# Loads of k, q and v of a pack-attention and soft-MoE kernel, issued as one transfer or as two

## The chip, the core and the metric

The kernel runs on one core of one Trainium2 chip. The metric is device time of one execution in microseconds (us). The kernel before takes 209.94 us (median of 3 runs, 209.9 to 210.69).

## What is computed

For each of 8 batches and 8 heads, with 576 rows of 64 numbers, 32 packing queries first attend to all keys and values, and then every row attends to the 32 packed results. The output, 4608 rows of 512 numbers, goes through a soft mixture of experts with 32 slots (8 experts of 4 slots).

```python
def sm_attn(qq, kk, vv):
    s = scale * np.matmul(qq, kk.transpose(0, 1, 3, 2))
    a = softmax(s)
    return np.matmul(a, vv)
p_packed = sm_attn(p, k, v)
x = sm_attn(q, p_packed, p_packed)          # then heads side by side: 4608 x 512
logits = x @ phi
slot_input = softmax(logits, axis=0).T @ x   # 32 slots
slot_out[e] = relu(slot_input[e] @ w1[e]) @ w2[e]
out = softmax(logits, axis=1) @ slot_out
```

All of it is in 32-bit floats.

## The kernel before

The attention is done in eight steps i, each for two batches (b2 = 0, 1) and four heads. A step needs six loads, two each of k, q and v, one for each b2. `rows9` (line 187) gives the source of such a load: head 4g + 2m + x, row 9r + t lies on partition 64x + r, at column 576m + 64t + d. So two heads (x) lie on the 128 partitions, two more (m) side by side in the columns, and each partition receives two runs of 576 numbers (2304 bytes), 294,912 bytes apart in memory. A load is 576 KB.

All loads stand in one list, `loads`, in the order p0; k, q, v of step 0; p1, p2, p3; k of step 1; four small pieces of phi; q and v of step 1; then k, q, v of steps 2 to 7; then the expert weights w1 and w2 (mostly 1024 KB each). `pump` (line 147) walks through this list as far as room allows and issues the transfers, all from SyncE (SP), whose queue is served in order. Most loads go into `ring`, a tile of 30,720 columns that is handed out from left to right and round again; a region is handed out again when its last reader has been recorded (`release`). `load` (line 136) issues one transfer for each load, at line 142; the pieces of phi are issued at line 151.

The order of all other work is written out by hand in `ORDER`, a list of tokens that name a function, a step and a part; each engine takes its instructions in that order. The tokens of this study: `kt` (line 395, VectorE) transposes a quarter of k of a step, and reads both halves m of the columns; `s1` (411) makes the first scores, and `mx1` (424) their maximum; `qp` (557) transposes q, in groups of columns 0 to 511, 512 to 639 and 640 to 1151; `ap` (444) transposes the first weights; `m` (466) multiplies by v, and reads both halves; `s2` (583), `mx2` (604) and `sb` (614) make the second scores, their maxima, and the difference; `p` (360) transposes the packing queries; `mp` (530) multiplies the packed results by phi; `w` (836) are products of ones that are not used, put into the order where TensorE would be idle. Steps overlap: `kt` of a step stands in the order among the second half of the step before.

Of the kernel before, what the change touches and what calls it, by code (L numbers as in the profile page):

```python
# [71 lines left out]
def pack_attention_soft_moe(  # L72
# [11 lines left out]
    nc = tc.nc  # L84

    B, H, S, D = q.shape
# [6 lines left out]
    T = S // R  # L93
# [42 lines left out]
    def load(dst, src):  # L136
        shape = src.shape[1:]
        if len(shape) == 2:
            dst = dst.rearrange("p (a b) -> p a b", a=shape[0])
        elif len(shape) == 3:  # L140
            dst = dst.rearrange("p (a b c) -> p a b c", a=shape[0], b=shape[1])
        nc.sync.dma_start(out=dst, in_=src)
# [4 lines left out]
    def pump():  # L147
        while state["next"] < len(loads):
            key, width, src = loads[state["next"]]
            if key == "phi":  # L150
                nc.sync.dma_start(out=width, in_=src)
                state["next"] += 1
                continue
            if key in spots:
                if spots[key] not in ready:
                    return
                dst = ready[spots[key]]
                where[key] = (dst, width)
                load(dst[:, 0:width], src)
                state["next"] += 1  # L160
                continue
            if "at" not in state:
                state["at"] = region(key, width)
            _, off, _ = state["at"]
            if not free(off, width):
                return
            regions.append(state.pop("at"))
            where[key] = (off, width)
            load(ring[:, off : off + width], src)
            state["next"] += 1  # L170
# [67 lines left out]
    for x in PLACE:  # L238
        key, width, src = extra.pop() if x == "x" else chunks.pop(0)
# [851 lines left out]
    for dd in range(ND):  # L1091
# [8 lines left out]
        for t in range(T):  # L1100
            n4, a = divmod(dd * T + t, 4)
# [57 lines left out]
```

## Time and profile before

| What | Before |
|---|---|
| Median of 3 runs | 209.94 us |
| The profiled execution | 211.11 us |
| its span (first to last instruction) | 209.0 us |
| TensorE busy (matmul) | 173.9 us, 83% of the span |
| VectorE, ScalarE, GpSimd busy | 125.4, 85.7, 39.1 us |
| Read from and written to memory | 62.46 MB, 9.44 MB |
| Share of the 16 DMA engines' time that the loads and stores took | 89.3% |

The profiled execution took 2.1 us more than its span, and 1.2 us more than the median. PE is TensorE's matmuls and PEld its weight loads; DVE is VectorE, ACT ScalarE, POOL GpSimd, SP SyncE. A releaser behind "<-" is what ended an idle time; "issue" is idle time in which the engine waited for nothing that the profile shows.

### The profile page before, as it was taken

The numbers are of one execution on the slowest core, as the hardware profiler recorded it, in microseconds if no ns is written. First come the engines' busy times: TensorE is split into PE (matmuls) and PEld (weight loads), VectorE is DVE, ScalarE is ACT, GpSimd is POOL, SyncE is SP. The second block draws the span as 40 slices with busy tenths as digits, with TensorE's granted clock in tenths as the row PEclk, the third lists the DMA queues.
The fourth block names the chain that finished last, engine by engine and source line by source line (L and its number), as shares of the span: only waits on it lengthen the run. The fifth ranks groups of instructions, "written<-read, shape, count | busy, mean of one in ns | idle before, by whom it ended". The sixth has DMA issues, their size and how long they took to land.

```text
span 209.0 us, 6539 instructions
## 1 busy us (share of the span) xinstructions
PE 173.9 (83%) x2827; PEld 110.1 (53%) x2827; DVE 125.4 (60%) x260; ACT 85.7 (41%) x205; POOL 39.1 (19%) x65
## 2 busy tenths in 40 slices
PE   7949779697898999999999998989989899796000
PEld 3625575593875858687858774543323323464000
DVE  1757488775749898977557799657742201387000
ACT  3063363394475847257377735031201000288000
POOL 7200006306442073002727001003000000000000
PEclk9999999999999999999999999999999999999555
DMA  6998999999999999955979999958999990069997
GB/s 210 386 383 283 395 393 391 389 389 389 389 390 391 388 396 405 408 205 182 346 292 389 408 407 420 420 219 278 427 425 422 419 384 14 3 265 411 410 417 302
DMA packets 23196, 72.31 MB, mean 346 GB/s; under 512 B 2176, under 2 KB 2944, under 8 KB 21248
## 3 DMA queue, kind: packets, MB, share of 16 engines
q1 hardware_dynamic: 23168, 71.90, 89.3%
q8 instruction: 22, 0.36, 0.7%
q14 instruction: 6, 0.05, 0.1%
HBM read 62.46 MB, written 9.44 MB: 344 GB/s over the span
## 4 chain that ended last, share of the span: by engine, by line
PE 60%; DVE 18%; ACT 8%; issue 7%; ACTq 0%; DVEq 0%
PE ps L583 9%; PE ps L466 7%; PE ps L836 7%; PE ps L1005 6%; PE ps L557 5%; PE ps L411 5%; PE ps L675 4%; PE ps L444 3%; ACT ring L345 3%; ACT work L345 2%; DVE mx L604 2%; PE ps L951 2%; DVE work L349 2%; PE ps L699 2%; DVE a L666 1%
## 5 line engine op out<-in xcount | busy, mean ns | idle before, releaser
L345 ACT COPY work<-ps 128x512 f32<-128x512 f32 (+3 forms) x64 | 28.9, 489 | 27.0 <-PE ps L557 12.8
L395 DVE STREAM_TRANSPOSE work<-ring 128x576 f32<-128x576 f32 x32 | 22.9, 752 | 2.8 <-DMA ring<-in_k_dram 2.6
L557 PE MATMUL ps<-ident,ring 128*128 128x128 f32 x144 | 20.8, 278 | 2.1 <-issue 1.9
L583 PE MATMUL ps<-work 128*64 128x64 f32 x576 | 20.1, 224 | 2.8 <-issue 2.4
L466 PE MATMUL ps<-ring,work 64*64 64x128 f32 x576 | 19.3, 274 | 2.2 <-ACT work L345 1.4
L583 PEld LDWEIGHTS ps<-work 128*64 128x64 f32 x576 | 18.4, 138 | 5.1 <-issue 3.9
L836 PE MATMUL ps<-ones 128*128 128x512 f32 (+3 forms) x40 | 19.2, 583 | 1.0 <-DVE ones L115 1.0
L466 PEld LDWEIGHTS ps<-ring,work 64*64 64x64 f32 x576 | 15.9, 133 | 5.2 <-ACT work L345 2.1
L557 PEld LDWEIGHTS ps<-ident,ring 128*128 128x128 f32 x144 | 15.9, 141 | 4.4 <-issue 3.1
L651 POOL TENSOR_TENSOR zt<-work 128x576 f32<-128x576 f32 x4 | 5.7, 1430 | 55.5 <-ACT work L643 55.5
L349 DVE COPY work<-ps 128x128 f32<-128x128 f32 (+3 forms) x28 | 13.0, 470 | 5.1 <-PE ps L557 1.9
L604 DVE TENSOR_REDUCE mx<-ps 128x36 f32<-128x1152 f32 x8 | 10.8, 1353 | 6.4 <-PE ps L583 6.2
L411 PE MATMUL ps<-work 32*32 32x288 f32 x512 | 13.4, 413 | 1.1 <-issue 0.9
L345 ACT COPY a2Tb<-ps 128x384 f32<-128x384 f32 x21 | 9.7, 481 | 10.8 <-PE ps L675 10.8
L427 ACT ACTIVATE work<-ps,nm 128x576 f32<-128x576 f32 x16 | 11.8, 741 | 4.5 <-DVE nm L424 4.5
L424 DVE TENSOR_REDUCE nm<-ps 128x2 f32<-128x1152 f32 x8 | 10.8, 1349 | 3.7 <-PE ps L411 3.7
L951 PE MATMUL ps<-ring,a2Tb 128*32 128x512 f32 x96 | 12.4, 594 | 0.4 <-DVE a2Tb L1017 0.4
L836 PEld LDWEIGHTS ps<-ones 128*128 128x128 f32 x40 | 7.2, 212 | 10.4 <-issue 9.2
L444 PE MATMUL ps<-ident,work 128*128 128x128 f32 x72 | 11.1, 277 | 1.5 <-ACT work L427 1.5
L1005 PE MATMUL ps<-ring,hT 128*32 128x512 f32 x88 | 11.4, 597 | 0.0
L345 ACT COPY ring<-ps 128x512 f32<-128x512 f32 (+1 forms) x21 | 10.4, 621 | 1.1 <-PE ps L1119 0.6
L654 POOL TENSOR_TENSOR zt<-zt 128x288 f32<-128x288 f32 (+2 forms) x18 | 10.5, 584 | 1.4
(138 smaller groups left out, 251.4 us busy)
## 6 DMA issues: line engine op xcount, KB each, us to landing
ring<-in_moe_w_dram SPq DMA_DIRECT2D x24, 1024.0 KB, 10.9
ring<-in_k_dram SPq DMA_DIRECT2D x16, 576.0 KB, 11.9
ring<-in_q_dram SPq DMA_DIRECT2D x16, 576.0 KB, 11.9
ring<-in_v_dram SPq DMA_DIRECT2D x16, 576.0 KB, 12.0
out_dram<-ring SPq DMA_DIRECT2D x10, 768.0 KB, 8.3
work<-in_moe_w_dram SPq DMA_DIRECT2D x6, 1024.0 KB, 11.2
a<-in_moe_w_dram SPq DMA_DIRECT2D x1, 1024.0 KB, 4.8
ring<-in_moe_w_dram SPq DMA_DIRECT2D x2, 512.0 KB, 18.0
```

The lines of the kernel that those rows point to most:

```text
L345: nc.scalar.copy(dst, src)
L349: nc.vector.tensor_copy(dst, src)
L395: nc.vector.transpose(kT[:, b2, :, c].rearrange("p m (t r) -> p m t r", t=T), view(f"k{i}.{b2}").rearrange("p (m t c d) -> p m t c d", m=2 ...
L411: nc.tensor.matmul(ps[32 * y : 32 * y + 32, banks["s1", i] + z, 0 : 32 * T], pT[rs, dd, b2, g, c, m], kT[rs, b2, m, c], start=(c == 0), st ...
L444: nc.tensor.transpose(ps[:, bank, o : o + P], a1[:, t].rearrange("p x r -> p (x r)"), ident)
L466: nc.tensor.matmul(ps[64 * b2 : 64 * b2 + 64, b + x, 0:P].rearrange("p (m d) -> p m d", m=2), a1T[rs, t, b2], view(f"v{i}.{b2}").rearrange ...
L557: nc.tensor.transpose(ps[:, bank, o : o + P], view(f"q{i}.{b2}")[:, P * n : P * n + P], ident)
L583: nc.tensor.matmul(psf[64 * b2 : 64 * b2 + 64, o + 64 * n : o + 64 * n + 64].rearrange("p (a s) -> p a s", a=2), qT[:, b2, n, 64 * x : 64 ...
L604: nc.vector.tensor_reduce(mxs[i % 2][:, a0:a1].rearrange("p a t -> p (a t)"), s2v(i, j).rearrange("p a t s -> p (a t) s"), axis=AX.X, op=A ...
L836: nc.tensor.matmul(ps[:, bank, 0 : P * n].rearrange("p (n c) -> p n c", n=n), ones, ones.unsqueeze(1).broadcast_to([P, n, P]), start=True, ...
L951: nc.tensor.matmul(ps[32 * a : 32 * a + 32, b + nh, :], xzf[:, (4 * e + a) * NSLOT : (4 * e + a + 1) * NSLOT], wv[:, j, nh * 512 : (nh + 1 ...
L1005: nc.tensor.matmul(ps[32 * a : 32 * a + 32, SO, :], hTf[:, (NJ * e + j) * NSLOT : (NJ * e + j + 1) * NSLOT], w2v(e, j), start=(e == 0 and ...
```

## The change

In `load`, a source of two rows of 576 numbers for each partition, which only the 48 loads of k, q and v have, is issued as two transfers, one for each m: 128 runs of 2304 bytes each, 288 KB, one behind the other in SP's queue. What is loaded, where it lies and the order of the list stay.

```diff
         if len(shape) == 2:
             dst = dst.rearrange("p (a b) -> p a b", a=shape[0])
+            if shape[0] == 2 and shape[1] == T * D:
+                for a in range(2):
+                    nc.sync.dma_start(out=dst[:, a], in_=src[:, a])
+                return
         elif len(shape) == 3:
             dst = dst.rearrange("p (a b c) -> p a b c", a=shape[0], b=shape[1])
         nc.sync.dma_start(out=dst, in_=src)
```

## Rows read from the trace of the kernel before

**Rows 1.** The page, parts 1 and 2: engines, and data moved in 40 slices.
```profile
PE 173.9 (83%) x2827; PEld 110.1 (53%) x2827; DVE 125.4 (60%) x260; ACT 85.7 (41%) x205; POOL 39.1 (19%) x65
...
GB/s 210 386 383 283 395 393 391 389 389 389 389 390 391 388 396 405 408 205 182 346 292 389 408 407 420 420 219 278 427 425 422 419 384 14 3 265 411 410 417 302
```

**Rows 2.** The chain that ended last, part of 18 to 56 us: start, us, what.
```profile
25.10 1.42 issue
...
29.53 1.32 DVE work L614
...
39.20 1.87 issue
...
47.59 0.90 issue
...
54.29 0.67 issue
```

**Rows 3.** Busy time and instructions (x) by stretch: us, PE, PEld, DVE, ACT, POOL.
```profile
41.00:48.48 7.48, 6.53 (x127) 5.61 (x127) 4.48 (x10) 5.59 (x12) 1.46 (x2) 1.00 1.05 387
48.48:54.95 6.47, 5.29 (x128) 3.73 (x128) 4.46 (x7) 2.78 (x8) 2.23 (x5) 1.00 1.05 390
```

**Rows 4.** The page, part 3: queue q8, its packets and MB.
```profile
q8 instruction: 22, 0.36, 0.7%
```

**Rows 5.** Packets by queue in the windows 48.49:52.30, 52.30:53.54, 91.0:94.24 and 94.24:95.6 us.
```profile
q1 hardware_dynamic: 682, 1.48, 104.8%
q14 instruction: 1, 0.01, 0.5%
...
q8 instruction: 1, 0.02, 6.2%
...
q1 hardware_dynamic: 80, 0.28, 22.5%
...
q8 instruction: 1, 0.02, 5.8%
```

**Rows 6.** PEld in order of time, near 93 us.
```profile
93.12 0.31 PEld L583 LDWEIGHTS ps<-work 128*64 128x64 f32 x6 [0.22 <-issue]
```

**Rows 7.** SP in order of time: start, us from first issue to end of the last.
```profile
0.73 0.38 SPq L142 DMA_DIRECT2D ring<-in_p_dram  x1
1.17 0.93 SPq L142 DMA_DIRECT2D ring<-in_k_dram  x2
...
14.26 1.25 SPq L151 DMA_DIRECT2D phi_sb<-in_moe_phi_dram  x2
15.55 1.11 SPq L142 DMA_DIRECT2D ring<-in_q_dram  x2
...
33.41 2.85 SPq L142 DMA_DIRECT2D ring<-in_k_dram  x2
```

**Rows 8.** Transfers issued at 0.73, 3.87, 18.82, 33.41, 154.27, 156.75 us: issue to landing.
```profile
DMA to landing us min/median/max: 2.1/2.1/2.1
...
DMA to landing us min/median/max: 10.4/10.4/10.4
...
DMA to landing us min/median/max: 8.6/8.6/8.6
...
DMA to landing us min/median/max: 12.0/12.0/12.0
...
DMA to landing us min/median/max: 18.6/18.6/18.6
...
DMA to landing us min/median/max: 17.4/17.4/17.4
```

**Rows 9.** DVE in order of time: the transposes of k of steps 2 and 4.
```profile
28.83 0.77 DVE L395 STREAM_TRANSPOSE work<-ring 128x576 f32<-128x576 f32 x1
...
51.21 1.43 DVE L395 STREAM_TRANSPOSE work<-ring 128x576 f32<-128x576 f32 x2
```

**Rows 10.** Waits that are instructions of their own at line 466: shortest, median, longest ns.
```profile
L466 PEldq EVENT_SEMAPHORE  x5: 51/51/2515, 13.1 to 114.1; - x5
```

## The prediction

> **What bounds the kernel now.** I read the page first. TensorE issues matmuls for 83% of the span, and from slice 5 to slice 17 (21 to 89 us) the DMA queue moves 388 to 408 GB/s without a break [rows 1]. Both look like bounds, so the next view is the chain that ended last. It runs mostly through TensorE, but in the stretch of k, q and v it holds four gaps named "issue", of 1.42, 1.87, 0.90 and 0.67 us, 4.86 us together [rows 2]: TensorE stands still and waits for no engine and no load. The stretches between gaps say why. From the second to the third there are 127 + 127 matmuls and weight loads, from the third to the fourth 128 + 128 [rows 3]: a gap comes every 256 instructions. Queue q8 brings 22 packets, 0.36 MB [rows 4], 16 KB each; TensorE's 2827 + 2827 instructions [rows 1] divided by 22 give 257. So these packets are TensorE's program, and the gaps are waits for it.
>
> How late is a packet? The third gap ends at 48.49 (47.59 + 0.90) [rows 2]. From there to 52.30 no q8 packet starts, while q1, the queue of the loads, is full; one starts in the window from 52.30 [rows 5], so 3.8 us pass. At 93.12 TensorE resumes after a short pause of the same kind, 0.22 us [rows 6]. There q1 runs empty, and the next q8 packet starts in the window from 94.24 [rows 5], 1.1 us later. So 2.7 us of the 3.8 are spent behind data. The gaps are a cost of a full load queue: what the change does to that queue counts more than what it does to any one load.
>
> **The change part by part.** *Issues.* 48 more, on SP alone. An issue takes SP 0.38 us, 0.44 from one start to the next [rows 7]. A load is 589,824 bytes, 1.51 us at the 390 GB/s of the full stretch [rows 3]; two issues fill 0.88 of that, and SP waits for the rest, so this costs 0. If that cover were gone, the second issue would delay its half by at most 0.44.
>
> *Depth of the queue.* A load lands 12.0 us after its issue [rows 8], eight times 1.51: eight are in flight, and a new one waits for the eighth before it. Halved transfers keep the count and halve the bytes, so 6.0 us of data are in flight instead of 12.1. The loads keep their rate if a new transfer gets going before those are gone; on an empty queue a transfer of 128 KB lands 2.1 us after its issue [rows 8]. I take 0. A shortfall would first show behind the small pieces of phi, below, and is bounded there.
>
> *The transfers themselves.* The rows of 2304 bytes stay, and there are 48 more transfers. The trace has no k load of 288 KB, so I bound it by the nearest: the two 512 KB loads of weights, issued at 154.27 and 156.75, land at 172.9 and 174.1 [rows 8], 1.2 us apart, 0.43 MB/us, like the 419 to 427 GB/s of slices 29 to 32, with 1024 KB loads [rows 1]. A price per transfer is thus under the rounding, 0.05 us: 0 to 2.4 us on the DMA queue over all 48. I take 0.5; it is hidden from step 4 on, whose k lands at 45.4 (33.41 + 12.0) and is first read at 51.21 [rows 8, 9].
>
> [...]
>
> *The pieces of phi.* This is the place where eight transfers that count as one each, large or small, matter. The third phi piece is issued at 14.26, q of step 1 at 15.55, so a piece takes 0.64 [rows 7]. With halves, the eighth transfer before the first piece is the second half of v of step 0, which lands at 14.3 (3.87 + 10.4) [rows 8]. All four pieces then come behind it, and q of step 1 at 14.3 + 4 x 0.64 = 16.9, 1.3 us later than now. The queue has run dry there already (283 GB/s in slice 4 [rows 1]), so the loads behind come 1.3 us later. k of step 2 lands at 27.4 (18.82 + 8.6) [rows 8] and then at 28.7; its first transpose starts at 28.83 [rows 9]. Cost 0, with 0.1 us to spare. The bounds: a landing of the second half 0.75 us earlier makes it 0 with more to spare, and a restart 1.7 us slower still, as in the rival below, costs 1.6.
>
> *Waits.* A reader of both halves waits for two transfers instead of one. That is at most 16 more waits on VectorE for k, 32 on TensorE for q and v, 51 ns each on TensorE's queue when nothing is awaited [rows 10], and VectorE's I count the same: 0 to 2.4 us. TensorE's are mostly taken ahead of the matmuls in flight; what they do cost is room among the 256 instructions of a packet: 32 x 6.47 us / 256 = 0.8 us where the program is the bound [rows 3]. That is so at the four gaps and at shorter pauses like the one at 93.12; I take 0.3.
>
> *The gaps.* The packet now waits 2.7 us behind data. With 6.0 us in flight, less the 0.75 that have just landed and about 1.8 (2.1 less 0.3 of data [rows 8]) until the replacement is there, an engine has some 3.5 us of data queued when it is the last of the 16, and less when it is ahead of the others. An estimate of 2 to 3.5 us stands against 2.7 now. The gain for a gap lies between 0 and 0.7; I take 0.35. The first gap gives nothing, because k of step 2 isn't there earlier. Three others: 1.0 us, of which other engines will take some; I count 0.8.
>
> **Sum:** 0.3 for waits less 0.8 for gaps, 0.5 us less. The profiled execution (211.11 us, span 209.0) would come to 210.6; the median of the runs stands 1.17 below it, so I predict 209.4. A measurement of this kernel can tell about 0.5%, 1.05 us, from no change; this is no change.
>
> **The rivals.** *The gaps close (faster).* If the wait behind data is counted in transfers and not in bytes, it halves or better: 2.7 becomes 1.35 or less. Then the second gap falls from 1.87 to 0.5, the third and fourth vanish; with the first held by k of step 2 the gain is 1.4 + 0.9 + 0.7 = 3.0 us, and shorter pauses beside: 209.9 less 3.0, plus 0.3 for waits, is 207.2, or 208.7 if half of it passes to the end, 206.5 if the short pauses go too. For it: the wait is constant where the queue is full, and gone where it is empty. Against it: the chain mixes in other waits at once. [...]
>
> *The restart after phi comes late (slower).* Beyond 1.4 us of delay, k of step 2 holds VectorE at 28.83, and the chain of waits passes through VectorE right behind (29.53) [rows 2]: each us of more delay is a us of time. If the stream comes 3 us late instead of 1.3, the cost is 1.6 us: 211.5 to 212. For it: 0.1 us to spare. Against it: 14.3 is the landing of the whole load, which the second half should not exceed.
>
> That the change does nothing can't be: the condition holds for all 48 loads and for no other.
>
> **How the numbers follow.** My forecast, no change, gets 0.47, the closing gaps 0.35, the late restart and other losses 0.18. The forecast's own range is 208.9 to 211.0. For 8 in 10 the range reaches into both rivals, down to 207.4 (a third of the faster case is left out) and up to 211.6. Faster by over 0.5%: 0.35; within: 0.47; slower: 0.18.
>
> **What would show it.** In the profile after: 96 issues of 288 KB for k, q and v, landing after 6 us in the full stretch; GB/s still near 390; q of step 1 issued near 16.9; the first transpose of k of step 2 near 28.8; gaps of "issue" still every 256 instructions, shorter by some 0.3 us. I am wrong if the gaps are gone (faster), or if VectorE waits for k of step 2 or 3 (slower).

## The result, and the profile after

The changed kernel takes 213.05 us (median of 4 runs, 212.32 to 213.16), beside 210.16 for the kernel before (4 runs, 209.90 to 210.69): a ratio of 1.0127, 95% interval 1.0095 to 1.0159. It is slower, by 2.9 us, and lies outside the predicted range, which ended at 211.6. In two later comparisons, on two chips and with 12 runs of the changed kernel each, the loss at the median was smaller and the times lay far apart: 212.04 against 211.19, and 212.52 against 211.11. By the ratio neither of these shows a loss: 1.0019 (0.9986 to 1.0053) and 0.9948 (0.9899 to 0.9998). A ratio counts only the runs within 1.5% of the fastest of their kernel; of kernels with halves up to 7 of 12 runs lie outside, so medians and ranges over all runs stand beside the ratios below.

The profiled execution took 213.16 us, with a span of 211.3, against 211.11 and 209.0. The page of the changed kernel, parts 1, 2 and 6 (the last: issues, KB each, us to landing):

```profile
PE 175.7 (83%) x2827; PEld 111.4 (53%) x2827; DVE 125.6 (59%) x260; ACT 85.8 (41%) x205; POOL 39.1 (18%) x65
...
PEclk9999979999999999999999999999999999999555
...
GB/s 191 386 364 194 390 397 368 386 388 388 375 390 389 390 390 402 407 304 37 356 404 316 413 405 423 419 243 268 423 420 423 419 407 21 3 280 409 414 419 267
...
ring<-in_k_dram SPq DMA_DIRECT2D x32, 288.0 KB, 5.9
```

What the change does is there: twice the issues, each landing after 5.9 us, about half of the 12.0 of before [rows 8]. The data rate of the full stretch is nearly what it was [rows 1]: slices 7 and 11 have 368 and 375 GB/s where the kernel before has 391 and 389, and the others are level, so the halves themselves cost the queue next to nothing. Two things are new: slice 4 has fallen from 283 to 194 GB/s, and in slice 6 (26.4 to 31.7 us) TensorE's granted clock is no longer full: 0.72 on the mean of the slice.

The chain that ended last has its "issue" gaps as before, but they are not the same ones [rows 2]. Start, us, what:

```profile
25.48 2.47 issue
...
41.13 0.92 issue
...
48.85 1.01 issue
...
62.71 1.33 issue
...
69.52 0.45 issue
```

The first gap has grown from 1.42 to 2.47 us. The second has halved, from 1.87 to 0.92. The fourth, of 0.67 near 54 us, is gone, and behind it stands a new one of 1.33 at 62.71. Part of the growth of the first gap is the kernel's own scatter: a second execution of the kernel before (e10_before_again) has 1.97 us there. The fences below show what follows the first gap: windows of the changed kernel (us, then PE, PEld, DVE, ACT and POOL busy, granted clock, DMA share, GB/s), and its matmuls in order of time.

```profile
27.00:28.00 1.00, 0.05 (x2) 0.05 (x2) 0.00 (x0) 0.00 (x0) 0.00 (x0) 1.00 1.04 403
28.00:29.00 1.00, 1.00 (x13) 0.93 (x13) 0.48 (x1) 0.00 (x0) 0.00 (x0) 0.88 1.05 394
29.00:30.00 1.00, 1.00 (x7) 1.00 (x6) 0.97 (x3) 0.65 (x2) 0.00 (x0) 0.50 1.07 396
...
31.00:32.00 1.00, 1.00 (x7) 1.00 (x6) 1.00 (x2) 0.57 (x2) 0.00 (x0) 0.50 1.07 392
32.00:33.00 1.00, 1.00 (x10) 0.93 (x8) 1.00 (x3) 0.60 (x2) 0.00 (x0) 0.92 1.01 383
```

```profile
28.50 1.23 PE L448 MATMUL ps<-ident,work 128*128 128x128 f32 x6
29.52 1.27 PE L561 MATMUL ps<-ident,ring 128*128 128x128 f32 x5
...
31.23 1.94 PE L561 MATMUL ps<-ident,ring 128*128 128x128 f32 x12
```

After 2.47 us of standing still TensorE gets a granted clock of 0.50, from shortly before 29 us until shortly after 32. The same transposes in the kernel before, at 1.00:

```profile
27.07 0.82 PE L444 MATMUL ps<-ident,work 128*128 128x128 f32 x6
27.72 0.71 PE L557 MATMUL ps<-ident,ring 128*128 128x128 f32 x5
...
28.60 1.47 PE L557 MATMUL ps<-ident,ring 128*128 128x128 f32 x12
```

Line numbers are 4 higher after the change. Matching the two traces matmul by matmul gives the lag of the changed kernel along the execution:

| Matmul starts, before and after (us) | Lag | What lies ahead of it |
|---|---|---|
| 7.67, 9.00 | 1.33 | first scores: second half of a k load of step 0 lands late |
| 15.69, 15.98 | 0.29 | other waits took most of it up |
| 26.52, 27.96 | 1.44 | first gap, 1.05 us longer |
| 28.92, 31.87 | 2.95 | a granted clock of 0.50 |
| 30.90, 33.10 | 2.20 | the wait for VectorE that the kernel before has here, 0.83 us, is covered |
| 41.07, 42.36 | 1.30 | second gap 0.95 shorter |
| 54.96, 55.47 | 0.51 | no fourth gap |
| 61.69, 64.04 | 2.36 | new gap, and longer matmuls right ahead of it |
| 191.00, 193.50 | 2.50 | the end |

What is late in this execution is thus not k, q or v behind phi, and not the rate of the stream, but a packet of TensorE's program in two places and the clock behind one of them.

How late is the packet behind the new gap? Counting 256 of TensorE's instructions from the end of the gap at 49.86 (48.85 + 1.01) leads to 55.30. From there, packets by queue in the windows 55.31:61.65 and 61.65:62.7:

```profile
q1 hardware_dynamic: 1188, 2.43, 104.6%
```

```profile
q1 hardware_dynamic: 192, 0.39, 99.6%
q8 instruction: 1, 0.02, 5.6%
```

No q8 packet for 6.3 us, then one at 61.66: a delay of 6.36, where the kernel before has 3.8 at the same instruction. TensorE resumes 2.4 us after a packet has started, behind this gap (64.04) as behind the third of before (46.06, then 48.49). This delay, from the 256th instruction to the start of the packet, is what the experiments are read by.

### The profile page after: what moved, and what is told of

It reads as the page before. It is cut to its first block, busy times and chain, and to the rows that moved or that the text cites. A ratio compares the mean times of both kernels' runs of the same rounds, so it can differ in the third digit from the quotient of the medians.

```text
span 211.3 us, 6629 instructions
## 1 busy us (share of the span) xinstructions
PE 175.7 (83%) x2827; PEld 111.4 (53%) x2827; DVE 125.6 (59%) x260; ACT 85.8 (41%) x205; POOL 39.1 (18%) x65
## 4 chain that ended last, share of the span: by engine, by line
PE 60%; DVE 15%; ACT 7%; issue 7%; DMA 3%; SPq 1%; ACTq 0%; DVEq 0%
PE ps L587 9%; PE ps L470 9%; PE ps L561 7%; PE ps L1009 6%; PE ps L415 5%; PE ps L840 4%; PE ps L448 4%; PE ps L679 4%; ACT ring L349 3%; DMA ring<-in_k_dram 3%; ACT work L349 2%; PE ps L955 2%; PE ps L703 2%; DVE a L670 1%; DVE work L353 1%
## 5 line engine op out<-in xcount | busy, mean ns | idle before, releaser
L349 ACT COPY work<-ps 128x512 f32<-128x512 f32 (+3 forms) x64 | 29.1, 489 | 28.7 <-PE ps L561 13.8
L561 PE MATMUL ps<-ident,ring 128*128 128x128 f32 x144 | 21.6, 288 | 0.2
L840 PE MATMUL ps<-ones 128*128 128x512 f32 (+3 forms) x40 | 18.6, 566 | 1.1 <-DVE ones L115 1.1
L561 PEld LDWEIGHTS ps<-ident,ring 128*128 128x128 f32 x144 | 16.9, 147 | 3.4 <-issue 2.2
L415 PE MATMUL ps<-work 32*32 32x288 f32 x512 | 14.4, 413 | 4.2 <-issue 2.3
L448 PE MATMUL ps<-ident,work 128*128 128x128 f32 x72 | 11.9, 291 | 1.5 <-ACT work L431 1.5
```

The source lines that it names most:

```text
L349: nc.scalar.copy(dst, src)
L415: nc.tensor.matmul(ps[32 * y : 32 * y + 32, banks["s1", i] + z, 0 : 32 * T], pT[rs, dd, b2, g, c, m], kT[rs, b2, m, c], start=(c == 0), st ...
L448: nc.tensor.transpose(ps[:, bank, o : o + P], a1[:, t].rearrange("p x r -> p (x r)"), ident)
L561: nc.tensor.transpose(ps[:, bank, o : o + P], view(f"q{i}.{b2}")[:, P * n : P * n + P], ident)
L840: nc.tensor.matmul(ps[:, bank, 0 : P * n].rearrange("p (n c) -> p n c", n=n), ones, ones.unsqueeze(1).broadcast_to([P, n, P]), start=True, ...
```

## The experiments

Whole loads and halves can be mixed by step, since the condition can ask for the step. Of each edit only the lines that matter are shown; `...` stands for the others, such as those that hand the name of a load to `load`. Runs are named by their labels; times are medians with the range of all runs. Runs that stand under one heading, and those that say so, shared a chip and the runs of the kernel before.

### Halves in a part of the steps, and phi placed singly

The first run (e1_first) keeps halves for steps 0 and 1 (the diff), the second (e2_rest) for steps 2 to 7 (with "not in"); the third and fourth move the pieces of phi, with halves everywhere (e3_spread_split) or whole loads (e4_spread_whole).

```diff
-            if shape[0] == 2 and shape[1] == T * D:
+            if shape[0] == 2 and shape[1] == T * D and key[1] in "01":
...
```
The list at step 1, first as it was and then as in the third and fourth run:

```
k1.0 k1.1 phi phi phi phi q1.0 q1.1 v1.0 v1.1
k1.0 phi k1.1 phi q1.0 phi q1.1 phi v1.0 v1.1
```

> Halves only for k, q and v of steps 0 and 1, whole loads from step 2. Theory A (the loss is made at the restart behind the pieces of phi: q of step 1 is issued 1.6 us later, k of step 2 lands 2.3 us later, the first program gap grows from 1.42 to about 2.5 us and TensorE's granted clock falls behind it): all of the loss of 2.9 us is here, 212.3 to 213.3. Theory B (halves delay the program packets all along the stretch of k, q and v, 3.9 us mean but up to 6.4): a third of the loss, 210.6 to 211.3. Theory C (19 more instructions on TensorE shift the places of the gaps): 210 to 211.

> Whole loads for steps 0 and 1, halves from step 2. Theory A: no change, 209.7 to 210.5, with the first gap near 1.42 us and the granted clock at 1.00 from 26 to 34 us. Theory B: two thirds of the loss, 211.5 to 212.5, gaps at 41 us and later longer or new ones. Theory C: most of the loss, 212 to 213, since most of the added waits come after step 1.

> Halves everywhere, but the four pieces of phi stand in the list singly, each behind a load of k or q of step 1, instead of all four between k and q. Theory A: q of step 1 is issued near 15.3 us instead of 17.2, slice 4 of the data rate rises from 194 to over 280 GB/s, k of step 2 lands near 27.5, the first gap and the clock dip are gone: 209.7 to 210.7. Theories B and C: little changes, 212 to 213.

> Whole loads everywhere, with the pieces of phi placed singly as in the run before. Theory A: the shorter restart of the kernel before (1.4 us of data lost in slice 4) goes too: 208.5 to 209.8. Theories B and C: no change, 209.7 to 210.5.

| Run | Median (range), us | Kernel before | Ratio (95%) |
|---|---|---|---|
| e1_first | 211.63 (210.94 to 212.45) | 211.21 (209.67 to 213.95) | 1.0018 (0.9990 to 1.0046) |
| e2_rest | 211.99 (209.08 to 214.90) | the same | 0.9995 (0.9952 to 1.0037) |
| e3_spread_split | 212.40 (208.93 to 216.02) | the same | 0.9993 (0.9950 to 1.0036) |
| e4_spread_whole | 210.17 (209.51 to 211.42) | the same | 0.9956 (0.9928 to 0.9985) |

Theory A, that the restart behind phi makes the loss, falls. e1_first has the late restart (254 GB/s in slice 4, q of step 1 issued at 16.62) and yet a first gap of 1.24 us, and its median is 0.4 us up, which can't be told from no change. It tests the restart in part only, since its k of step 2 comes whole and lands at 28.33, 0.9 us later than before, where the halves of the changed kernel land 2.3 us later. e3_spread_split has the early restart (q issued at 14.97, slice 4 at 293 GB/s) and still loses 1.2 us at the median. In e2_rest there is no late restart at all, the first load of k of step 2 has landed by 25.57 (27.43 before), and the late packet near 61 us is there (table below). What goes with the loss is halves from step 2 on, and they bring something beside a higher median: ranges of 5.8 and 7.1 us in 12 runs each, where e1_first and e4_spread_whole have 1.5 and 1.9 in 12 and the kernel before 4.3 in 35. The numbers expected were set from a kernel before at 210.2, which takes 211.2 on this chip: e1_first lies between the ranges of theories A and B, and e4_spread_whole, though faster, inside that of B and C.

e4_spread_whole was made to test theory A's other side, and is faster than the kernel before. The data rate no longer sags in slice 4 (283 before):

```profile
GB/s 215 382 380 378 391 391 391 391 390 391 389 392 391 388 400 405 406 142 199 348 279 400 412 411 413 422 202 306 430 421 426 419 381 10 3 276 405 416 416 303
```

### The changed kernel again, the depth alone, the instructions alone

The second of these (e6_depth) has whole loads, and an unread transfer behind each from step 2 on, which takes up places in flight. The third (e7_grid) has whole loads and one unused matmul in each step; the trace shows each as two matmuls and two weight loads.

```diff
         nc.sync.dma_start(out=dst, in_=src)
+        if len(shape) == 2 and shape[0] == 2 and shape[1] == T * D and key[1] not in "01":
...
+            nc.sync.dma_start(out=tiny[:, o : o + 4], in_=src[0:16, 0, 0:4])
...
```
```diff
+        if j == 0:
+            nc.tensor.matmul(
+                ps[0:32, b, P : P + 1], ones[0:32, 0:32], ones[0:32, 0:1], start=True, stop=True
+            )
         for t in range(*tk(j)):
```

> The changed kernel again, beside the kernel before, on one chip with more runs. Theory A (one loss, at the restart behind phi, each time the same): 212.5 to 213.5 with a spread no wider than that of the kernel before. Theory B (halves scatter the delay of program packets, so that luck decides how many gaps come and whether the clock falls behind them): median 212 to 213, a spread of 4 us or more, twice that of the kernel before; the profile again shows packet delays from 2 to 6 us or more where whole loads give 3.2 to 4.0.

> Whole loads; from step 2 on each is followed by a transfer of 256 bytes that nobody reads. It takes one of the eight places in flight, so four whole loads are in flight, 6 us of data as with halves, while loads and their rows stay whole. Theory B1 (scatter comes from the small depth, 6 us in flight): packet delays from 2 to 6 us as with halves, a gap near 64 us, spread of runs as with halves from step 2 (209 to 215), median 211 to 212.5. Theory B2 (scatter comes from the transfers being halves): delays 3.2 to 4.0 us as before, the four gaps of before, median within 0.5 us of the kernel before.

> Whole loads; in each of the eight steps TensorE gets one more matmul of one column with its weight load, not used, ahead of the products with v: 16 more instructions, against 19 in the changed kernel. Theory C (the loss comes from more instructions on TensorE, which shift the places at which packets are awaited): 211.5 to 213. Theories A and B: the 16 instructions cost 0 to 0.8 us, 209.9 to 211 where the kernel before has 210.2, and packet delays stay at 3.2 to 4.0 us.

| Run | Median (range), us | Kernel before | Ratio (95%) |
|---|---|---|---|
| e5_after_again | 212.04 (210.38 to 214.22) | 211.19 (209.23 to 212.70) | 1.0019 (0.9986 to 1.0053) |
| e6_depth | 210.52 (208.18 to 212.08) | the same | 0.9951 (0.9911 to 0.9991) |
| e7_grid | 211.58 (210.29 to 213.40) | the same | 1.0026 (0.9993 to 1.0060) |

e5_after_again: neither quite. The spread is 3.8 us, near theory B's 4, and nearly as wide for the kernel before on this chip (3.5). e7_grid was meant to add 16 instructions; its trace has 28 more on TensorE's queue than the kernel before (16 matmuls and 16 weight loads more, 4 others fewer), the changed kernel 19. They cost 0.4 us, under what can be told from no change, and bring no late packet (3.94 us near 61 us); theory C is too small. e6_depth is the telling one. Its loads land after 6 us, like halves, but whole:

```profile
ring<-in_k_dram SPq DMA_DIRECT2D x16, 576.0 KB, 6.5
```

The 11 packets from 24 to 90 us come 2.6 to 4.1 us after the 256th instruction, and of the gaps in the chain over 0.5 us two are left:

```profile
24.42 2.20 issue
...
40.06 1.60 issue
```

So six us of data in flight do not make packets late. Here they come earlier (a mean of 3.40 us over these 11, against 3.74 in the kernel before), and the kernel is 0.7 us faster at the median, though the ranges overlap; the stream is also below its full rate at times (319 to 390 GB/s in slices 7 to 11), and the two were not separated. Theory B1 falls. B2 expected the delays and the four gaps of before, which is not what came, but its main point stays: at the full rate of the stream, packets of over 5.5 us came only with halves.

### Both gains together, 3 us in flight, and the kernel before once more

e8_spread_depth joins the edits of e4_spread_whole and e6_depth. e9_half_small has halves from step 2 on with an unread transfer behind each; e10_before_again is the kernel before.

```diff
+            for a in range(2):
+                nc.sync.dma_start(out=dst[:, a], in_=src[:, a])
...
+                nc.sync.dma_start(out=tiny[:, o : o + 2], in_=src[0:16, 0, 0:2])
...
```

> Whole loads, with the pieces of phi placed singly and, from step 2 on, an unread transfer of 256 bytes behind each load: both edits that were faster than the kernel before by themselves (ratios 0.9956 and 0.9951). If their gains come from different places (slice 4 of the stream, and the delay of packets from step 2 on), they add: ratio 0.989 to 0.993. If both only shorten the same gaps: 0.994 to 0.997.

> Whole loads for steps 0 and 1; from step 2 on halves, each followed by an unread transfer of 128 bytes, so that four halves are in flight, 3 us of data. Theory B3 (a packet waits behind the data in flight on its engine, up to 6 us with halves; the late packets of 5.7 to 7.1 us met the engine that was last): no delay above 4.2 us, no gap near 64 us, spread of runs as with whole loads, median at or under 211 unless the data rate falls below 385 GB/s. Theory B4 (late packets belong to halves, whatever is in flight): delays of 5 us and more stay, 211.5 to 213. If 3 us is too little for the stream, slices 6 to 15 of the data rate show 300 to 370 GB/s and VectorE waits for k: 213 to 220.

> The kernel before once more, for a second profile of it. If delays with whole loads are regular whatever the execution, they are again 3.2 to 4.0 us but for the one near 46 us with 5.0; gaps near 26, 41, 48 and 55 us of 0.5 to 2.2 us.

e9_half_small takes 224.62 us (222.40 to 226.33) against 211.18, a ratio of 1.0582 (1.0525 to 1.0639), more than the 213 to 220 expected for a stream that runs short. Its page, parts 2 and 6:

```profile
GB/s 211 400 361 376 312 257 269 268 262 219 267 303 265 265 264 281 246 257 309 371 415 410 408 404 405 414 422 405 398 419 423 420 417 159 0 185 414 409 416 272
...
ring<-in_k_dram SPq DMA_DIRECT2D x24, 288.0 KB, 4.1
```

Four halves in flight move 219 to 303 GB/s in slices 7 to 16, some 265: 3 us of data can't cover 4.1 us from issue to landing. But the packets behind the first gap now come after 0.9 to 3.3 us, and none of the later gaps is left. That agrees with theory B3, that a program packet's delay hangs on the data in flight; but the stream is also far below its full rate here, and which of the two shortens the delay isn't shown. The price of getting there this way is the stream. e10_before_again (210.68 us) has the delays of the first profile again (3.18 to 4.06, and 5.01 for the one near 46 us): with whole loads they repeat. e8_spread_depth: 211.27 (208.05 to 213.16), ratio 0.9924 (0.9871 to 0.9976); the median says that little was gained, so it was run again, below.

### Where the load is cut

To keep the transfers, waits and issues of halves but nearly the size of a whole load, e11_uneven cuts by partitions, 120 and 8; e12_parts cuts 64 and 64. e13_rest_again is e2_rest once more, beside them.

```diff
-            for a in range(2):
-                nc.sync.dma_start(out=dst[:, a], in_=src[:, a])
+            for rs in (slice(0, 120), slice(120, P)):      # e12: 64 for 120
+                nc.sync.dma_start(out=dst[rs], in_=src[rs])
...
```

> Whole loads for steps 0 and 1; from step 2 on each load is cut into 120 and 8 of its partitions, 540 and 36 KB. Transfers, waits of the readers and issues of SP are as many as with halves, 6 us of data are in flight; only the sizes differ. If the waits and instructions that come with two transfers make the loss (theory C): packet near 61 us at 5.7 to 7.1 us of delay, times as with halves from step 2, 211.5 to 212.5, spread 4 us or more. If it is the equal halves (B2): delays 2.5 to 4.2 us as in the run with four whole loads in flight, no gap near 64 us, 210 to 211.

> As the run before, but cut into 64 and 64 partitions, 288 KB each, two rows of 2304 bytes for each partition. If two equal parts are the cause, wherever they are cut: a late packet of 5.7 us or more, 211.5 to 212.5 and a spread of 4 us or more, as with halves from step 2. If it is the cut by heads m: delays at or under 4.2 us, 210 to 211.

> Halves from step 2 on once more, on the chip of the two runs before: 211.5 to 212.5 with a spread of 4 us or more, and again a packet of 5.7 us or more near 61 us with a gap behind it.

As tests of the waits both failed, since they changed something far larger: 235.41 us (229.81 to 239.80) and 231.34 (218.24 to 236.19) against 210.85. The page of e12_parts, parts 2 and 6:

```profile
GB/s 208 393 348 381 221 231 230 235 235 239 232 236 241 245 260 265 284 283 290 313 408 405 408 408 405 409 424 391 314 423 428 418 421 242 0 128 412 415 414 268
...
ring<-in_k_dram SPq DMA_DIRECT2D x24, 288.0 KB, 9.8
```

288 KB on 64 partitions move at 221 to 245 GB/s (slices 5 to 14), where 288 KB on 128 partitions mostly move at 386 to 390. The cut into 120 and 8 partitions moves 231 to 264 GB/s in the same slices. Why either cut is so slow, no run here says. Packets come later in e12_parts (4.5 to 7.25 us from 20 to 90 us) but not in e11_uneven (1.0 to 5.2), with as many bytes in flight; this too stays open.

e13_rest_again: 211.82 (209.05 to 215.12) against 210.85 (210.18 to 213.43). Its chain and its windows (columns as above):

```profile
24.39 2.43 issue
...
40.21 1.77 issue
...
61.49 1.90 issue
```
```profile
62.00:64.00 2.00, 0.60 (x19) 0.20 (x19) 0.00 (x0) 0.00 (x0) 1.04 (x3) 1.00 1.04 392
64.00:66.00 2.00, 2.00 (x46) 0.86 (x37) 1.58 (x3) 0.48 (x1) 0.00 (x0) 0.63 1.07 395
66.00:68.00 2.00, 2.00 (x18) 0.73 (x17) 1.03 (x3) 0.73 (x2) 0.00 (x0) 0.52 1.03 386
```

The late packet (6.87 us) and the new gap are back, and behind this gap too TensorE's granted clock falls: 0.63 and 0.52 on the mean of the last two windows, which by estimate is 0.50 from 64.5 to 67.9 us.

### The changed kernel a third time, beside the two faster versions

> The changed kernel a third time. If the loss is a fixed cost of 2 to 3 us (theory A): 213 to 214 with a spread of 2 us. If it is mostly chance (theory B2: late packets with halves): 211.5 to 212.5, 4 us or more from the fastest to the slowest, a packet delay of 5.7 us or more near 61 us with a gap of 0.8 to 2.2 us behind it.

> Whole loads with the pieces of phi placed singly, again: 0.5 to 1.3 us under the kernel before (209.5 to 210.5), spread under 3 us, no packet delay above 5.3 us.

> The same with the unread transfers of 256 bytes from step 2 on, again: if four whole loads in flight are a gain of their own, 208.5 to 210 and under the run before by 0.5 us or more; if its first ratio of 0.9924 was luck of its wide spread, level with the run before or above it.

| Run | Median (range), us | Kernel before | Ratio (95%) |
|---|---|---|---|
| e14_after_third | 212.52 (209.05 to 215.03) | 211.11 (209.79 to 213.75) | 0.9948 (0.9899 to 0.9998) |
| e15_spread_again | 210.26 (209.80 to 212.12) | the same | 0.9966 (0.9928 to 1.0004) |
| e16_spread_depth_again (6 runs) | 209.92 (207.03 to 212.22) | the same | 0.9861 (0.9786 to 0.9936) |

The 12 runs of the changed kernel fall into five from 209.05 to 210.52 and seven from 212.38 to 215.03, with nothing between. The profiled execution of e14 (210.32 us) is one of the five. Its chain, from 20 to 72 us, gaps over 0.4 us:

```profile
25.16 1.92 issue
...
40.26 1.84 issue
...
66.49 0.48 issue
```

There is no gap near 62. The 256th instruction is at 54.24, the packet at 57.18, a delay of 2.94. The same program with the same halves has the late packet in one execution and not in another. The six profiled executions with halves from step 2 on, beside each other:

| Execution | Delay near 61 us | Gap behind it | First gap | Stretches at a granted clock of 0.50 up to 70 us | Time, us |
|---|---|---|---|---|---|
| e14_after_third | 2.94 | none | 1.92 | once | 210.32 |
| e5_after_again | 5.71 | 0.78 | 1.92 | none | 210.96 |
| e2_rest | 6.16 | 1.35 | 1.70 | once, near 17 us | 211.83 |
| e13_rest_again | 6.87 | 1.90 | 2.43 | twice | 212.99 |
| the changed kernel | 6.36 | 1.33 | 2.47 | once | 213.16 |
| e3_spread_split | 7.06 | 2.15 | 1.91 | twice | 213.43 |

In the executions with whole loads (the kernel before twice, e1_first, e4, e6, e7, e8, e15, e16) this delay is 2.6 to 3.9 us, and no gap follows. The fall of the clock to 0.50 is no mark of halves: it came as well, once each, in five of these nine, behind gaps of 2.15 us (e1), 1.86 (e4), 2.20 (e6), 1.85 (e7) and 1.86 (e15), and e4 and e15 stand below the kernel before at the median all the same.

Every run's mean granted clock is on record too. In the 12 runs of e14 it is 0.960 to 0.970 in the five and 0.940 to 0.956 in the seven. In the kernel before on that chip the ten of 23 runs under 210.7 us have 0.960 to 0.970 and the six of 212.2 us and more 0.948 to 0.951. So with whole loads as with halves, much of the spread goes with the clock. The clock isn't all of the loss: in e5_after_again the median clock is no lower than that of the kernel before beside it (0.964 against 0.961), and the median time is 0.9 us longer.

So two things vary with halves from run to run: whether one packet comes late, which whole loads never showed there, and how often the clock falls, which they show too. That late packets make the loss is seen matmul by matmul in the one execution above; for the other runs it rests on the company in the table, and a version of the halves without late packets, which would prove it, wasn't found.

What stays open is why a packet can wait 6 us and more with halves and not with whole loads in the same depth. If a packet waits behind data, nearly all of the 6 us in flight would have to stand ahead of it, and which of the 16 DMA engines served a packet isn't in the trace. The waits that come with two transfers were not tried within whole loads at full rate; e7_grid added instructions to TensorE, but no waits.

The best version is whole loads with phi placed singly: in both comparisons under the kernel before, by 1.0 and 0.9 us at the median (the second interval just reaches 1), with the narrowest spread. With the unread transfers added it has the fastest runs of all (207.03) and better ratios, but scatters as much as halves do.

## Why the prediction was wrong

The step that failed is **the gaps**: "I take 0.35 [...] I count 0.8" of gain, between 0 and 0.7 for each gap. It took the packet's delay for one number, 3.8 us, that less data in flight could only lower. Its own working left room for more: an estimate of "2 to 3.5 us stands against 2.7 now" reaches 0.8 us above what it had, and the loss that this allows has no term. Nor was the delay one number before: over the ten packets from 20 to 90 us it runs from 3.17 to 5.00. Where it looked, it was right in part: the second gap fell by 0.95 and the fourth by 0.67 (the third grew by 0.11), and e6_depth, which has the depth without halves, gains 0.7 us at the median. But with halves the delay scatters, from 1.7 to 7.1 us between 20 and 90 us, about the same mean (3.5 to 3.9). Early packets gain little, for a packet that is in time can't be more than in time; a late one costs its whole excess. Here that was 1.05 us at the first gap, 1.33 at a new one, and 1.7 more at a granted clock of 0.50 behind the first, of which 0.9 was taken up at the next wait. The clock has no term in the sum, although a gap of 1.87 stood in the rows [rows 2]; there it stayed at 1.00 [rows 3].

- **Issues and transfers**: as forecast. Halves cost the stream next to nothing: slices 9, 12 and 13 show 388 to 390 GB/s, 389 to 391 before [rows 1]. 288 KB on all partitions move about as fast as 576.
- **Depth**: as forecast, 5.9 us to landing (6.0), rate kept. Half of it again would not have been enough (e9_half_small).
- **The pieces of phi**: q of step 1 was forecast at 16.9 and is issued at 17.16. Start, us from first issue to end of the last, on SP:

```profile
14.46 2.66 SPq L155 DMA_DIRECT2D phi_sb<-in_moe_phi_dram  x4
17.16 2.02 SPq L142 DMA_DIRECT2D ring<-in_q_dram  x4
...
21.19 2.95 SPq L142 DMA_DIRECT2D ring<-in_k_dram  x4
```

  The mechanism was right, but the term of 0 came out by luck. The second half of the first load of k of step 2, issued at 22.00, lands 7.8 us later at 29.76, not at 28.7: 2.3 us later than before, where the forecast had 1.3 and room for 1.4. With VectorE there at 28.83, as before [rows 9], this would have cost some 0.9 us by the prediction's own reckoning. But TensorE's first gap had held up VectorE too, its transposes start 1.4 us later, and there is no wait for data ahead of them:

```profile
30.27 0.78 DVE L399 STREAM_TRANSPOSE work<-ring 128x576 f32<-128x576 f32 x1
```

- **Waits**: at the products with v the waits that are instructions of their own go from 5 [rows 10] to 17 (shortest, median, longest ns); TensorE's queue has 19 instructions more in all, not the 32 allowed for:

```profile
L470 PEldq EVENT_SEMAPHORE  x17: 51/51/1367, 14.4 to 117.4; - x17
```

  With the price of 0.3 us for all waits, e7_grid's 0.4 for 28 instructions agrees within what can be told.
- **Step 0**, which the sum left out: the transposes of k of its second batch wait for data until 8.17, those of before only until 6.84:

```profile
8.17 1.44 DVE L399 STREAM_TRANSPOSE work<-ring 128x576 f32<-128x576 f32 x2 [1.48 <-DMA ring<-in_k_dram]
```

  The first scores start 1.33 us later, and by 15.98 all but 0.29 of it is taken up. e1_first, with halves in steps 0 and 1 alone, puts the start and the restart together at 0.4 us.
- **The rivals**: the late restart named the right side, and more delay came than its 1.4 us, but no wait for k came of it, and e2_rest and e3_spread_split have their late packets without it. The closing gaps had something to them: three of four shrank or went in e6_depth. Neither of the two signs that were to prove the forecast wrong (gaps gone, VectorE waiting for k of steps 2 or 3) came; the loss came through the gaps themselves.

The size of 2.9 us is that of the first comparison, whose four runs of the changed kernel have a mean granted clock of 0.948 to 0.959. The medians on two other chips give 0.9 and 1.4 us, and the ratios there no loss at all, so its size stays open; that it depends on how often a late packet comes, and on the clock, fits the runs but isn't measured.

## What to carry to other kernels

Where an engine waits for its program, look at the spread of the packets' delays and not only at their mean: with about the same mean, one late packet cost over 1 us here, and a gap can cost twice, once as idle time and again as matmuls at a granted clock of 0.50 (1.05 and 1.7 us at the first gap). When an estimate reaches to both sides of today's value, put both into the sum. Before loads are cut into more transfers, count what they take of the places in flight: the four small pieces of phi, standing together, left slice 4 with 283 GB/s, and with 194 under halves; placed singly among big loads they left it with 378, and that gained about 1 us here without any halves. If a load is to be cut, cut it so that each part still covers all 128 partitions; the two here that did not, 120 and 8 and 64 and 64, took 235.41 and 231.34 us against 210.85.

## What the runs showed of the hardware beside this

- The granted clock fell to 0.50 behind gaps of 2.47 us here, 2.43 and 1.90 in e13_rest_again, 1.92 in e14_after_third, and with whole loads behind 1.85 in e7_grid and 1.86 in e4_spread_whole. Behind 1.87 and 1.97 in the two executions of the kernel before and 1.92 in e5_after_again it stayed at 1.00, so idle time alone didn't decide it.
- A transfer of the same 288 KB took 5.9 us to land on 128 partitions and 9.8 on 64, and the stream went from 390 to some 235 GB/s.
- With half the data in flight (whole loads, 6 us instead of 12) program packets came 0.3 us earlier on average and the ratio was 0.9951 (0.9911 to 0.9991), though the stream was often below its full rate (319 to 390 GB/s in slices 7 to 11): the shallower queue of loads was not slower here.
